# Three weight tiles in place of one, and a later start with a closer spacing for the norms of chunk 3, in a kernel that computes attention and a gated linear unit side by side

## The chip, the cores and the metric

The kernel runs on one core of a Trainium2 chip. The metric is the device time of one execution in microseconds (us). Before the change it is 309.67 us, the median of three runs (309.5, 309.67 and 310.33). In the profile, PE is TensorE's matmul row, PEld its weight loads, DVE is VectorE, ACT is ScalarE, POOL is GpSimd, and SP is SyncE, which here only issues DMAs.

## What is computed

There are 2048 rows `x` of width 640, in bf16. The rows are normalised, and two branches that both read the normalised rows are added to `x`:

```python
xn = layernorm(x)                      # (x - mean) / sqrt(var + 1e-5)
q, k, v = split(xn @ wqkv)             # 32 heads of width 20
p = softmax(mask(q @ k.T * 20**-0.5))  # causal, window of 256 positions
a = (p @ v) @ wo
b = (sigmoid(xn @ w_gate) * (xn @ w_up)) @ w_down   # inner width 1536
out = x + a + b
```

## The kernel before

**Tiling.** The 2048 positions are four chunks of 512 (chunks 0 to 3), each of four row blocks of 128. For one chunk the work is: the norms (DVE and POOL), which leave four row blocks `xn` (L273); the turning of each `xn` into the transposed tile `xnT` (four DMA transposes from SP's queue, L284; for chunk 0 it is done on PE, L280); the Q and K products (L300), whose results go to scratch in DRAM (`st`, L308) and come back spread over partitions (L318); the V products (L329); the scores and their exponentials (L490, L496), masks on POOL (L507) and, in one step of five, on DVE (L500, tile `edge`); the products with V (`acc`, L523); the GLU's gate and up products (`pg` L414, `pu` L421), whose tanh is on ACT (L417) and whose product `h` is on DVE (L425); and the output stage `g_out`, which for each row block adds twelve products of `h` with `w_down` (L435) and five with `wo` (L442) for either half of the columns (`y`), adds the row block of `x` on DVE (`rows`, L446) and stores it (L457).

**Order.** Instructions are issued on each engine in the order in which the Python program emits them. The main loop goes through the steps of the scores. Between two steps it pulls other work from a list, `fill`, whose entries (L692 to L710) are generators: each `yield` hands back the PE nanoseconds that were just emitted, and the loop goes on pulling until a budget (`APART`, 1800 ns, with a credit) is used up. `mix(a, b, first, every)` puts one pull of generator `b` behind every `every`-th yield of `a`, from yield number `first` on. The planner counts only the costs that `a` yields, so pulls of `b` at cost 0 do not change which PE work is emitted where.

**The norms.** `g_norms(c, turn)` (L346) emits the statistics of four row blocks, one per pull, then three pulls that emit nothing, then four `xn`, one per pull. For chunk 3 `turn` is false, and the transposes are a generator of their own, `g_turns(3)`, behind the norms. Chunk 3's norms begin in the entry `gu1b` (L704), which computes the GLU products 7 to 11 of chunk 1: ten yields, so ten pulls, four with statistics, three empty, three with an `xn`. The fourth `xn` and the four transposes come in `out1` (L705), the output stage of chunk 1, at every third yield. In the middle of its first row block `out1` also computes the first GLU product of chunk 2. The entry behind `out1` is `qk3`, the first that reads the transposed tile of chunk 3.

**The weights.** Q, K and V weights are one tile `wqkv` of 128 partitions by 5 by 1920 (L142). Four DMAs fill it: V's two halves (`load_v`, L159), then Q and K (`load_wqkv`, L150). PE's weight load for the second product of the first Q block waits for the load of K; the products of K have no wait on a DMA. 

Quoted lines, from `g_norms` and from the list:

```python
        for _ in range(3):
            yield 0
...
    norms3 = g_norms(3, False)
...
    fill.add("gu1b", mix(g_gu(1, 7, 12), norms3, 0, 1, False), 5 * GU)
    fill.add("out1", mix(g_out(1, g_gu(2, 0, 1)), itertools.chain(norms3, g_turns(3)), 1, 3), OUT + GU)
    fill.add("qk3", g_qk(3), 50 * MM)
```

PSUM tiles of one bank (`pg`, `pu`, `y`, `acc`, `pqk`, `pv`) share four buffers, `ps_d`; SP's DMAs go through one queue, in order of their issue.

Of the kernel before, what the change touches and what calls it, by code (L numbers as in the profile page):

```python
# [9 lines left out]
P = 128  # L10
S = 2048
D = 640
# [3 lines left out]
DC = D // P  # L16
# [9 lines left out]
HALF = 320  # L26
# [11 lines left out]
BF16 = mybir.dt.bfloat16  # L38
# [55 lines left out]
def kernel(  # L94
# [11 lines left out]
    nc = tc.nc  # L106
# [4 lines left out]
    def pool(name, bufs, **kw):  # L111
        return ctx.enter_context(tc.tile_pool(name=name, bufs=bufs, **kw))

    const = pool("const", 1)
# [24 lines left out]
        xc[c] = t  # L139
        nc.sync.dma_start(out=t, in_=xr[:, c * SBC:(c + 1) * SBC, :])  # L140

    wqkv = const.tile([P, DC, 3 * D], BF16, name="wqkv")  # L142
    wqkv_r = A_wqkv.rearrange("(c p) n -> p c n", p=P)
    wg = [const.tile([P, DC, FS], BF16, name=f"wg{k}") for k in range(F // FS)]
    wu = [const.tile([P, DC, FS], BF16, name=f"wu{k}") for k in range(F // FS)]
# [2 lines left out]

    ones = nc.const_aps.tensor(1.0, [P, CW], BF16)
    def load_wqkv(part):  # L150
        nc.sync.dma_start(out=wqkv[:, :, part * D:(part + 1) * D],
                          in_=wqkv_r[:, :, part * D:(part + 1) * D])

    xc[0] = xp.tile([P, SBC, D], BF16, name="xc")

# [1 line left out]
        queue.dma_start(out=xc[0][:, s, :], in_=xr[:, s, :])  # L157

    def load_v(hf):  # L159
        a = 2 * D + hf * HALF  # L160
        nc.sync.dma_start(out=wqkv[:, :, a:a + HALF], in_=wqkv_r[:, :, a:a + HALF])

    load_rows(0, nc.sync)
    load_rows(1, nc.sync)
    load_rows(3, nc.sync)
    load_v(0)
    load_rows(2, nc.sync)
    load_v(1)
    load_wqkv(0)
    load_wqkv(1)  # L170

    scratch = {(w, k): tc.dram_tile([H * 32, CW], BF16, name=f"s{w}{k}")
# [89 lines left out]
    def ln_block(c, s, mv=None):  # L262
        return ln_mv(ln_half(c, s, 1, ln_half(c, s, 0)), mv)

    def rstd_blocks(mvs):
        rstds = lnp.tile([P, SBC], FP32, name="rstds", bufs=1)
        nc.gpsimd.tensor_scalar(out=rstds, in0=mvs[:, :, 1], scalar1=EPS, scalar2=None, op0=ADD)
        nc.gpsimd.tensor_tensor(out=rstds, in0=rstds, in1=neghalf, op=POW)
        return rstds

    def norm_block(c, s, mv, rstd):
        xn = lnp.tile([P, D], BF16, name="xn")
        nc.vector.tensor_scalar(out=xn, in0=xc[c][:, s, :], scalar1=mv[:, 0:1],  # L273
                                scalar2=rstd[:, 0:1], op0=SUB, op1=MULT)
        xns[c, s] = xn
# [7 lines left out]
    def turn_block(c, s):  # L283
        nc.sync.dma_start(out=xnT[c][:, :, s * P:(s + 1) * P], in_=xns.pop((c, s)), transpose=True)  # L284

    def new_xnT(c):
        xnT[c] = xtp.tile([P, DC, CW], BF16, name="xnT")


    qk = {}  # L290
    vt = {}

    def proj_block(w, c, m):


        base = 0 if w == "q" else D
        ps = ps_d.tile([P, CW], FP32, name="pqk", tag="d")
        for d in range(DC):
            wt = wqkv[:, d, base:base + D].rearrange("p (k m) -> p m k", m=DC)
            nc.tensor.matmul(ps, lhsT=wt[:, m, :], rhs=xnT[c][:, d, :],  # L300
                             start=(d == 0), stop=(d == DC - 1))
        st = stp.tile([P, CW], BF16, name="st")
        if w == "q":
            nc.vector.tensor_copy(out=st, in_=ps)
        else:
            nc.scalar.copy(out=st, in_=ps)
        dst = scratch[w, c % 2].rearrange("(h j) s -> h j s", j=32)
        nc.sync.dma_start(out=dst[:, 4 * m:4 * m + 4, :], in_=st)  # L308
# [17 lines left out]
    def project_v(c, s, hf, home=ps_d, tag="d"):  # L326
        ps = home.tile([P, CW], FP32, name="pv", tag=tag)
        for d in range(DC):
            nc.tensor.matmul(ps[:, 0:HALF], lhsT=xnT[c][:, d, s * P:(s + 1) * P],  # L329
                             rhs=wqkv[:, d, 2 * D + hf * HALF:2 * D + (hf + 1) * HALF],  # L330
                             start=(d == 0), stop=(d == DC - 1))
        return ps

# [7 lines left out]
    def proj_v(c, s, hf, copy):  # L341
        copy_v(c, s, hf, project_v(c, s, hf), copy)

    MM = 216

    def g_norms(c, turn):  # L346


        new_xnT(c)
        mvs = lnp.tile([P, SBC, nc.vector.BN_AGGR_DIM], FP32, name="mvs", bufs=1)  # L350
        for s in range(SBC):
            ln_block(c, s, mvs[:, s, :])
            if s == SBC - 1:
                rstds = rstd_blocks(mvs)
            yield 0
        for _ in range(3):
            yield 0
        for s in range(SBC):
            norm_block(c, s, mvs[:, s, :], rstds[:, s:s + 1])
            yield 0  # L360
            if turn:
                turn_block(c, s)

    def g_turns(c):
        for s in range(SBC):
            turn_block(c, s)
            yield 0

    def g_qk(c):
        for w in "qk":  # L370
            for m in range(DC):
                proj_block(w, c, m)
                if c == 0 and w == "q" and m == 1:
                    load_x(1)
                if c == 0 and w == "q" and m == 3:
                    load_gu(wu, B_w_up, 0, FS // 2)
                if c == 1 and w == "q" and m == 3:
                    load_wo()
                if c and w == "k" and m == 1:
                    spread("q", c, 0, GH)  # L380
                yield 5 * MM
        if c == 0:
            spread("q", c, 0, 2)
            spread("k", c, 0, 2)
            spread("q", c, 2, 4)
            spread("k", c, 2, 4)
# [19 lines left out]
    def part(w, d, f):  # L406
        k, first = divmod(f * P, FS)
        return w[k][:, d, first:first + P]

    def g_gu(c, f0, f1):  # L410
        for f in range(f0, f1):
            pg = ps_d.tile([P, CW], FP32, name="pg", tag="d")
            for d in range(DC):
                nc.tensor.matmul(pg, lhsT=part(wg, d, f), rhs=xnT[c][:, d, :],  # L414
                                 start=(d == 0), stop=(d == DC - 1))
            th = tp.tile([P, CW], FP32, name="th")
            nc.scalar.activation(out=th, in_=pg, func=TANH, scale=0.5)  # L417
            yield 5 * MM
            pu = ps_d.tile([P, CW], FP32, name="pu", tag="d")
            for d in range(DC):  # L420
                nc.tensor.matmul(pu, lhsT=part(wu, d, f), rhs=xnT[c][:, d, :],  # L421
                                 start=(d == 0), stop=(d == DC - 1))
            h = hp.tile([P, CW], BF16, name="h")
            ht[c, f] = h
            nc.vector.scalar_tensor_tensor(out=h, in0=th, scalar=1.0, in1=pu, op0=ADD, op1=MULT)  # L425
            yield 5 * MM
# [6 lines left out]
    def down(c, s, y, cut):  # L433
        for f in range(FC):
            nc.tensor.matmul(y[:, 0:cut[1] - cut[0]], lhsT=ht[c, f][:, s * P:(s + 1) * P],  # L435
                             rhs=wd[:, f, cut[0]:cut[1]], start=(f == 0), stop=False)
            if f % 6 == 5:
                yield 6 * 136
# [11 lines left out]
    def new_rows(c, s, name="rows", bufs=3, queue=nc.sync):  # L450
        rows = lnp.tile([P, D], BF16, name=name, bufs=bufs)
        queue.dma_start(out=rows, in_=xr[:, c * SBC + s, :])
        return rows
# [5 lines left out]
    def outp(c, s, ys, rows):  # L459
        for y, cut in zip(ys, HALVES):  # L460
            add_wo(c, s, y, cut)
        for y, cut in zip(ys, HALVES):
            add_x(y, cut, rows)
        store(c, s, rows)

    def g_out(c, between, ahead=()):
        nxt = new_rows(c, 0)
        for s in range(SBC):
            rows = nxt
            if s == 0:  # L470
                yield from ahead
            if s + 1 < SBC:
                nxt = new_rows(c, s + 1)
            ys = [ps_d.tile([P, CW], FP32, name=f"y{i}", tag="d") for i in range(2)]
            for y, cut in zip(ys, HALVES):
                yield from down(c, s, y, cut)
            if s == 0:
                yield from between
            outp(c, s, ys, rows)
            yield 10 * 136  # L480
# [117 lines left out]
    def mix(a, b, first, every=1, rest=True):  # L598

        for k, cost in enumerate(a):  # L600
            yield cost
            if k >= first and (k - first) % every == 0:
                yield next(b, 0)
        if rest:
            yield from b
# [74 lines left out]
    fill = Fill()  # L680
    GU = 10 * MM
    OUT = 4 * 34 * 136
    APART = 1800
    FIRST_PART = 1000
    def later(load, *args):
        load(*args)
        yield 0

    norms1 = g_norms(1, True)
    norms2 = g_norms(2, True)  # L690
    norms3 = g_norms(3, False)
    fill.add("gu0a", mix(g_gu(0, 0, 4), norms1, 4, 1, False), 4 * GU)  # L692
    fill.add("gu0b", mix(g_gu(0, 4, 12), norms1, 0), 8 * GU)
    fill.add("x2", later(load_x, 2), 0)
# [7 lines left out]
    fill.add("qk2", g_qk(2), 50 * MM)  # L702
    fill.add("v2", mix(g_v(2), g_gu(1, 3, 7), 0, 1), 40 * 136 + 4 * GU)
    fill.add("gu1b", mix(g_gu(1, 7, 12), norms3, 0, 1, False), 5 * GU)  # L704
    fill.add("out1", mix(g_out(1, g_gu(2, 0, 1)), itertools.chain(norms3, g_turns(3)), 1, 3), OUT + GU)  # L705
    fill.add("qk3", g_qk(3), 50 * MM)
    fill.add("v3", mix(g_v(3), g_gu(2, 1, 5), 0, 1), 40 * 136 + 4 * GU)
    fill.add("gu2", g_gu(2, 5, 12), 7 * GU)
# [38 lines left out]
    c = NCH - 1  # L747
# [62 lines left out]
```

## Time and profile before

| What | Value |
|---|---|
| runs | 309.5, 309.67, 310.33 us |
| the profiled execution | 309.64 us |
| its span, from the first to the last instruction | 307.9 us |
| outside the span | 1.7 us |
| granted TensorE clock, mean | 1.000 |
| busy share of the span: PE, DVE, ACT, POOL | 98%, 56%, 64%, 55% |
| output stage of chunk 1 on PE (`out1`) | from 153.43 to 178.39 us |
| first Q product of chunk 3 on PE | 178.74 us |

A page of the profile gives busy time and instructions of each engine, the span in 40 slices, the chain of work that ended last (followed back from the last instruction), and groups of instructions by line with what ended the idle time in front of them. The timeline view merges neighbouring instructions of one line; its columns are the start, the length of the merged piece, engine, line, operation, tiles, count, and in brackets the idle time in front with its releaser. The modelled end of a matmul lies after the start of the next one, so lengths of PE pieces are best read from start to start.

### The profile page before, as it was taken

How to read it: one execution, taken by the hardware profiler on the slowest of the kernel's cores; microseconds unless marked ns; L12 is line 12 of the kernel's file. 1: busy time of each engine (PE TensorE's matmuls, PEld its weight loads, DVE VectorE, ACT ScalarE, POOL GpSimd, SP SyncE). 2: the span in 40 equal slices, each digit the busy share in tenths (PEclk: the TensorE clock that was granted, in tenths of full speed). 3: DMA queues.
4: the chain of work that ended last, by engine and by line, in shares of the span. 5: the costliest groups of instructions: out<-in, count | busy, mean ns of one | idle time of the engine just before them, and what ended most of it. 6: DMA issues, size and time to landing. Idle time of an engine off the chain costs nothing.

```text
span 307.9 us, 9937 instructions
## 1 busy us (share of the span) xinstructions
PE 300.4 (98%) x4276; PEld 167.7 (54%) x4311; DVE 171.2 (56%) x339; ACT 198.4 (64%) x197; POOL 168.7 (55%) x308
## 2 busy tenths in 40 slices
PE   7999999999999999999999999999999999999995
PEld 3654444555657654554457654554546664444774
DVE  4633667648698364487946164383734536363523
ACT  6923877698854649888674547878585547688000
POOL 6000686687874828576672728457372937566000
PEclk9999999999999999999999999999999999999999
DMA  7997986984709363630015312650000200000202
GB/s 220 366 319 237 333 161 199 351 228 144 234 2 127 69 179 124 189 109 2 3 24 87 87 57 87 209 162 0 3 2 2 86 27 21 2 2 6 84 21 67
DMA packets 40460, 35.68 MB, mean 116 GB/s; under 512 B 10560, under 2 KB 39872, under 8 KB 40384
## 3 DMA queue, kind: packets, MB, share of 16 engines
q1 hardware_dynamic: 39552, 34.27, 38.6%
q10 hardware_dynamic: 864, 0.77, 0.8%
q8 instruction: 34, 0.56, 0.8%
q14 instruction: 10, 0.08, 0.1%
HBM read 23.63 MB, written 10.26 MB: 110 GB/s over the span
## 4 chain that ended last, share of the span: by engine, by line
PE 96%; issue 1%; DMA 1%; ACT 1%; DVE 0%; SPq 0%
PE y L435 18%; PE pu L421 17%; PE pg L414 17%; PE pqk L300 14%; PE ps L490 9%; PE pv L329 7%; PE y L442 7%; PE acc L523 6%; DMA xc<-in_A_x_dram 1%; PE pt L280 0%; ACT xn L620 0%; ACT xn L625 0%; DVE xn L631 0%; SPq L157 0%; ACT rstd L626 0%
## 5 line engine op out<-in xcount | busy, mean ns | idle before, releaser
L507 POOL TENSOR_SCALAR_AFFINE_SELECT pT<-pT 64x512 bf16<-64x512 bf16 (+1 forms) x256 | 157.1, 614 | 109.1 <-ACT pT L496 96.6
L496 ACT ACTIVATE pT<-ps 128x2048 bf16<-128x2048 f32 (+1 forms) x76 | 141.0, 1855 | 59.8 <-PE ps L490 57.9
L425 DVE SCALAR_TENSOR_TENSOR h<-th,pu 128x512 bf16<-128x512 f32 x48 | 32.8, 683 | 51.4 <-PE pu L421 44.9
L421 PE MATMUL pu<-xnT,wu 128*128 128x512 bf16 x228 | 59.0, 380 | 0.7 <-issue 0.2
L414 PE MATMUL pg<-xnT,wg 128*128 128x512 bf16 x226 | 58.5, 380 | 0.9 <-issue 0.3
L435 PE MATMUL y<-wd,h 128*128 128x320 bf16 (+2 forms) x396 | 56.8, 295 | 0.0
L300 PE MATMUL pqk<-xnT,wqkv 128*128 128x512 bf16 x191 | 45.4, 381 | 0.6 <-issue 0.2
L435 PEld LDWEIGHTS <-h 128*128 128x128 bf16 x396 | 36.7, 98 | 15.9 <-issue 1.8
L417 ACT ACTIVATE th<-pg 128x512 f32<-128x512 f32 x48 | 28.6, 595 | 15.5 <-PE pg L414 15.4
L414 PEld LDWEIGHTS <-wg 128*128 128x128 bf16 x240 | 22.3, 98 | 25.8 <-issue 2.0
L421 PEld LDWEIGHTS <-wu 128*128 128x128 bf16 x240 | 22.0, 98 | 25.5 <-issue 2.0
L300 PEld LDWEIGHTS <-wqkv 128*128 128x128 bf16 x200 | 22.5, 119 | 18.7 <-issue 1.4
L535 DVE STREAM_TRANSPOSE t<-acc 128x512 f32<-128x512 f32 x32 | 21.1, 696 | 20.1 <-PE acc L523 20.1
L490 PE MATMUL ps<-qT,kT 20*64 20x320 bf16 (+4 forms) x1440 | 32.1, 260 | 0.0
L490 PEld LDWEIGHTS <-kT 20*64 20x64 bf16 x1440 | 15.4, 103 | 24.9 <-issue 21.8
L446 DVE SCALAR_TENSOR_TENSOR rows<-y,rows 128x320 bf16<-128x320 f32 x30 | 14.4, 488 | 25.9 <-PE y L442 25.7
L547 DVE TENSOR_TENSOR on<-t,rec 128x320 bf16<-128x320 f32 (+4 forms) x48 | 27.8, 579 | 1.1
L329 PE MATMUL pv<-wqkv,xnT 128*128 128x320 bf16 x160 | 25.8, 300 | 0.0
L442 PE MATMUL y<-wo,oc 128*128 128x320 bf16 (+2 forms) x165 | 24.2, 295 | 0.0
L338 DVE CAST v<-pv 64x320 bf16<-64x320 f32 x29 | 14.1, 486 | 12.5 <-PE pv L329 12.3
L523 PE MATMUL acc<-pT,v 64*32 64x320 bf16 (+4 forms) x1440 | 19.7, 253 | 0.0
L523 PEld LDWEIGHTS <-v 64*32 64x32 bf16 x1440 | 16.2, 91 | 5.8 <-ACT pT L496 1.7
(48 smaller groups left out, 157.3 us busy)
## 6 DMA issues: line engine op xcount, KB each, us to landing
qT<-sq SPq DMA_DIRECT2D x16, 256.0 KB
kT<-sk SPq DMA_DIRECT2D x16, 256.0 KB
sq<-st SPq DMA_DIRECT2D x20, 128.0 KB
sk<-st SPq DMA_DIRECT2D x20, 128.0 KB
out_dram<-rows SPq DMA_DIRECT2D x15, 160.0 KB
wg<-in_B_w_gate_dram SPq DMA_DIRECT2D x4, 480.0 KB
wu<-in_B_w_up_dram SPq DMA_DIRECT2D x4, 480.0 KB
xc<-in_A_x_dram SPq DMA_DIRECT2D x3, 640.0 KB
```

Of the source, the lines that this page charges most:

```text
L300: nc.tensor.matmul(ps, lhsT=wt[:, m, :], rhs=xnT[c][:, d, :], start=(d == 0), stop=(d == DC - 1))
L329: nc.tensor.matmul(ps[:, 0:HALF], lhsT=xnT[c][:, d, s * P:(s + 1) * P], rhs=wqkv[:, d, 2 * D + hf * HALF:2 * D + (hf + 1) * HALF], start=( ...
L414: nc.tensor.matmul(pg, lhsT=part(wg, d, f), rhs=xnT[c][:, d, :], start=(d == 0), stop=(d == DC - 1))
L417: nc.scalar.activation(out=th, in_=pg, func=TANH, scale=0.5)
L421: nc.tensor.matmul(pu, lhsT=part(wu, d, f), rhs=xnT[c][:, d, :], start=(d == 0), stop=(d == DC - 1))
L425: nc.vector.scalar_tensor_tensor(out=h, in0=th, scalar=1.0, in1=pu, op0=ADD, op1=MULT)
L435: nc.tensor.matmul(y[:, 0:cut[1] - cut[0]], lhsT=ht[c, f][:, s * P:(s + 1) * P], rhs=wd[:, f, cut[0]:cut[1]], start=(f == 0), stop=False)
L442: nc.tensor.matmul(y[:, 0:cut[1] - cut[0]], lhsT=oc[c, m][:, s * P:(s + 1) * P], rhs=wo[:, m, cut[0]:cut[1]], start=False, stop=(m == DC - 1))
L490: nc.tensor.matmul(ps[a * U:(a + 1) * U, i, col * U:(col + n) * U], lhsT=qk["k", kc, o // GH][32 * i:32 * i + DH, o % GH + a, kb * U:(kb + ...
L496: nc.scalar.activation(out=pt[:, :, 0:width], in_=ps[:, :, 0:width], func=EXP, scale=SCALE)
L507: nc.gpsimd.affine_select(out=view, in_=view, pattern=[[0, HG], [0, n], [sign, U]], compare_op=GE, fill=0.0, base=base, channel_multiplier ...
L523: nc.tensor.matmul(acc[32 * i:32 * i + 32, q * U:(q + n) * U], lhsT=vt[kb][a * U:(a + 1) * U, u, h * VW:h * VW + 32], rhs=pt[a * U:(a + 1) ...
```

## The change

Two things are changed. `g_norms` gets a parameter for the number of empty pulls between statistics and `xn`; chunk 3 uses 6 instead of 3, and `out1` pulls from chunk 3's norms and transposes at every second yield instead of every third. And the weights of Q, K and V become three tiles `wq`, `wk`, `wv` of 128 by 5 by 640, filled by the same four DMAs in the same order.

```diff
-    wqkv = const.tile([P, DC, 3 * D], BF16, name="wqkv")
+    wqkv = [const.tile([P, DC, D], BF16, name="w" + part) for part in "qkv"]
...
     def load_wqkv(part):
-        nc.sync.dma_start(out=wqkv[:, :, part * D:(part + 1) * D],
-                          in_=wqkv_r[:, :, part * D:(part + 1) * D])
+        nc.sync.dma_start(out=wqkv[part], in_=wqkv_r[:, :, part * D:(part + 1) * D])
...
-        a = 2 * D + hf * HALF
-        nc.sync.dma_start(out=wqkv[:, :, a:a + HALF], in_=wqkv_r[:, :, a:a + HALF])
+        a = hf * HALF
+        nc.sync.dma_start(out=wqkv[2][:, :, a:a + HALF], in_=wqkv_r[:, :, 2 * D + a:2 * D + a + HALF])
...
-            wt = wqkv[:, d, base:base + D].rearrange("p (k m) -> p m k", m=DC)
+            wt = wqkv["qk".index(w)][:, d, :].rearrange("p (k m) -> p m k", m=DC)
...
-                             rhs=wqkv[:, d, 2 * D + hf * HALF:2 * D + (hf + 1) * HALF],
+                             rhs=wqkv[2][:, d, hf * HALF:(hf + 1) * HALF],
...
-    def g_norms(c, turn):
+    def g_norms(c, turn, gap=3):
...
-        for _ in range(3):
+        for _ in range(gap):
             yield 0
...
-    norms3 = g_norms(3, False)
+    norms3 = g_norms(3, False, 6)
...
-    fill.add("out1", mix(g_out(1, g_gu(2, 0, 1)), itertools.chain(norms3, g_turns(3)), 1, 3), OUT + GU)
+    fill.add("out1", mix(g_out(1, g_gu(2, 0, 1)), itertools.chain(norms3, g_turns(3)), 1, 2), OUT + GU)
```

## The prediction

> **What bounds the kernel.** I read the page's busy shares first, then the chain that ended last, then the groups, and then only the stretch around `out1` in the chain, the timeline and the waits. On the page:
>
> ```profile
> PE 300.4 (98%) x4276; PEld 167.7 (54%) x4311; DVE 171.2 (56%) x339; ACT 198.4 (64%) x197; POOL 168.7 (55%) x308
> ...
> PE 96%; issue 1%; DMA 1%; ACT 1%; DVE 0%; SPq 0%
> ...
> L300 PE MATMUL pqk<-xnT,wqkv 128*128 128x512 bf16 x191 | 45.4, 381 | 0.6 <-issue 0.2
> L435 PEld LDWEIGHTS <-h 128*128 128x128 bf16 x396 | 36.7, 98 | 15.9 <-issue 1.8
> ```
>
> PE is 96% of the chain, and nearly all of its groups have no idle time in front that anything but "issue" ends. So the kernel is bound by PE from about 7 us on, and an edit that leaves PE's instructions alone can gain only where PE waits. The instruction lists of the two kernels show PE in the same order, matmul for matmul. What changes is: on DVE the place of the four `xn` of chunk 3; on SP the place of their four transposes; and one wait on PE, that for the load of K. The question is thus where PE waits for these three.
>
> The chain through the start of `out1`:
>
> ```profile
> 153.50 1.60 PE y L435 x11
> 155.10 0.04 issue
> 155.14 1.12 PE y L435 x7
> ```
>
> Twelve products make one `y`, and the break is in front of the twelfth: it needs the last `h` of chunk 1. DVE's timeline there, and the weight load:
>
> ```profile
> 152.63 0.65 DVE L425 SCALAR_TENSOR_TENSOR h<-th,pu 128x512 bf16<-128x512 f32 x1
> ...
> 152.78 0.59 ACT L417 ACTIVATE th<-pg 128x512 f32<-128x512 f32 x1
> ...
> 153.20 1.30 DVE L273 TENSOR_SCALAR xn<-xc,mvs,rstds 128x640 bf16<-128x640 bf16 x2
> ...
> 154.42 0.67 DVE L425 SCALAR_TENSOR_TENSOR h<-th,pu 128x512 bf16<-128x512 f32 x1
> 155.01 1.41 DVE L273 TENSOR_SCALAR xn<-xc,mvs,rstds 128x640 bf16<-128x640 bf16 x2
> 155.14 0.79 PEld L435 LDWEIGHTS <-h 128*128 128x128 bf16 x7 [0.38 <-DVE h L425]
> ```
>
> Two `xn` stand ahead of that `h` on DVE. It ends at 154.42 + 0.67 = 155.09, and PE goes on at 155.14. How long PE lost is read from start to start, against the same 18 products followed by scores in the third row block:
>
> ```profile
> 153.43 2.84 PE L435 MATMUL y<-wd,h 128*128 128x320 bf16 x18
> 156.20 0.42 PE L490 MATMUL ps<-qT,kT 20*64 20x320 bf16 x16
> ...
> 168.13 2.62 PE L435 MATMUL y<-wd,h 128*128 128x320 bf16 x18
> 170.67 0.42 PE L490 MATMUL ps<-qT,kT 20*64 20x320 bf16 x16
> ```
>
> 156.20 - 153.43 = 2.77 us here, 170.67 - 168.13 = 2.54 us there: 0.23 us.
>
> **The norms on DVE.** The new order is: both last `h` of chunk 1, two `xn`, the `h` of chunk 2, the third `xn`, the two `rows` of the first row block, the `edge` mask, the fourth `xn`. The last `h` now only needs its tanh, done at 152.78 + 0.59 = 153.37, and ends near 153.4 + 0.67 = 154.1. The twelfth product wants it at 153.43 + 11 x 0.136 = 154.93 (0.136 is 2.46 us / 18, the 18 products from 174.48 to 176.94). So it is 0.8 us early, and the stall of **0.23 us** goes. All later times of PE move up by that much; nothing else is late at this place, because the next waits on DVE (`y` banks) are further on.
>
> The first two moved `xn` fall into idle DVE time: the profile shows 3.39 us idle in front of the `h` at 159.81. The third now stands between that `h` and the `rows`. Before: `h` 159.81 to 160.50, `rows` at 160.88 and 161.56, to 162.05, `edge` from 162.04 to 162.46. After, with 0.23 taken off: `h` to 160.27, `xn` to 160.93 (660 ns, the mean of its group) or 161.18 (906 ns, its longest), first `rows` to 161.42 or 161.67, second to 161.9 or 162.16, `edge` no later than 162.6. Behind these `rows` wait the banks of the `acc` products, which start at 163.08 - 0.23 = 162.85, and `edge` is read later within them. Even the longest `xn` leaves 0.7 us, so I cost it at **0**; cover gone, it would cost PE what an `xn` has over 0.66 + 0.95, about 1.6 us. Below nothing it cannot go, as PE does not wait there. The fourth `xn` lies in front of a wait for `acc` that idles DVE 1.95 us: **0**.
>
> **The transposes on SP.** Before, they are issued at these places:
>
> ```profile
> 153.85 1.23 SPq L284 DMA_TRANSPOSE xnT<-xn  x1
> 162.08 0.36 SPq L457 DMA_DIRECT2D out_dram<-rows  x1
> 162.49 0.41 SPq L452 DMA_DIRECT2D rows<-in_A_x_dram  x1
> 162.96 2.54 SPq L284 DMA_TRANSPOSE xnT<-xn  x2
> 168.69 0.34 SPq L457 DMA_DIRECT2D out_dram<-rows  x1
> 169.08 0.43 SPq L452 DMA_DIRECT2D rows<-in_A_x_dram  x1
> 169.56 1.21 SPq L284 DMA_TRANSPOSE xnT<-xn  x1
> ```
>
> After: store, load, transpose 1, store, transpose 2, load, transposes 3 and 4, store, store. The second store waits for `rows` and goes at 168.46; transpose 2 is issued from 168.9 to 170.1, the load of the last row block to 170.5, transposes 3 and 4 to 173.1 (1.23 each, with gaps). The load comes 1.0 us later than before and is read at 177.82, so that is hidden. For the landing, the trace's DMA completion records: the pair issued from 162.96 to 165.50 landed at 165.78 and 168.13, 2.63 us behind the end of its issue; the single one of 169.56 landed at 172.40, 1.6 behind. So the fourth lands by 173.1 + 2.6 = 175.7 us. `qk3` starts at 178.74 - 0.23 = 178.5. Slack 2.8 us, cost **0**; past it every us costs one. Before, this slack was 6.3 us (178.74 - 172.40), so the change uses up more than half of it.
>
> Here a page of the Trainium skill speaks against the change. "VectorE: DVE Perf Modes", section "The three transpose paths", gives 1309 ns for a DMA transpose of 128 by 128 bf16; our tiles have five such blocks, an estimate by that page of 6.5 us each if the blocks go one after the other, and the last of three from 168.9 would land near 188.5, ten us late. The trace disagrees: the second of the pair landed 2.35 us behind the first. The sum goes by the rows.
>
> **The weights.** The wait for K moves from the second product of Q to the first of K, 25 products or 25 x 0.216 = 5.4 us later on PE. In this execution it held nothing: K had landed at 12.83 (completion records), the first Q product started at 13.20, and the group of L300 shows no idle time that a DMA ended. Gain **0**, and if K landed late in an execution, up to 5.4 us of lateness would now be hidden; no row shows that it does. Same weight loads, same products, same bytes; a load's rows in SBUF now lie side by side instead of 3,840 bytes apart. No row shows what that is worth. From above: PE's first V product starts at 6.96 and the first Q product at 13.20; 40 V products (5.44 us) and two turns by PE (8.40 to 8.68, 10.80 to 11.08: 0.56) fill 6.0 of these 6.24, so faster loads gain at most 0.24. From below: Q's 800 KB landed 2.3 us ahead of K's (10.53, 12.83); if V's two halves, 800 KB together, took a quarter longer, the first products would start 0.6 late. I take 0, since the packets are as many and as long, which is the nearest row (the same four loads, before).
>
> **Sum.** 309.64 (the profiled execution; 307.9 of span and 1.7 around it) - 0.23 + 0 + 0 + 0 = **309.41 us**. The profiled execution lies 0.03 below the median of the runs, 309.67.
>
> **Rivals.** A: the forecast, 309.4. B: the gain is given back or not made: the last `h` is held by something else, or the third `xn` delays the banks. For it, DVE is dense up to 154.4; against it, 0.8 and 0.7 us of slack. Time: **309.64**. C, the slower one: the transposes arrive late at `qk3`. Three of them are now issued behind the store of the second row block; it decides from the point where each takes over (178.5 - 168.9) / 3 = 3.2 us. Rows: 2.35 and 2.63 us speak against it. At twice the row, 4.7 us each, the last lands at 168.9 + 14.1 = 183.0, 4.5 late: **313.9**. C is the case that the Trainium skill's figure above speaks for; by that page's estimate the time would be 309.4 + 10 = about 319. D: the loads at the start go differently: **309.2** to **310.0** (309.41 - 0.24, 309.41 + 0.6). The change doing nothing that it says is B.
>
> **How the numbers follow.** A 0.62, B 0.21, C 0.07, D 0.07, and 0.03 for a gain that no view explains. 0.3% is 0.93 us, about what a measurement of this kernel can tell from no change: A, B and most of D are within it, C is slower, and 0.01 of D with it. So faster 0.03, same 0.89, slower 0.08. The range takes A, B, D's near part, and the spread of the runs of before below and above (309.5 to 309.67, once 310.33): 309.0 to 310.1.
>
> **What would show it.** Right: in the changed profile the first 18 products of `out1` take 2.54 us from start to start, the weight load of `h` has no wait for DVE, `acc` starts without a wait behind the third `xn`, and `qk3`'s first product without one for `xnT`. Wrong: a DMA-ended idle time at L297 at the start of `qk3` (C), a stall in front of `acc` (B), or a first V product well off 6.96 us (D).

## The result, and the profile after

The changed kernel takes 309.31 us (median of eleven runs, 309.01 to 310.45), the kernel before 310.21 us in the same comparison (eleven runs, 309.5 to 310.73). The ratio is 0.9975, 95% interval 0.9964 to 0.9986: a gain of 0.78 us, between 0.43 and 1.12, where 0.23 was forecast. (The medians alone are 0.90 us apart.)

The profiled execution of the changed kernel took 309.91 us, more than that of before (309.64). So the gain cannot be read from the two spans, and the places have to be compared one by one. From its page:

```profile
PE 300.0 (97%) x4276; PEld 167.5 (54%) x4311; DVE 170.7 (55%) x339; ACT 198.4 (64%) x197; POOL 168.7 (55%) x308
...
PE 96%; DMA 1%; issue 1%; DVE 1%; ACT 0%; SPq 0%
...
L297 PE MATMUL pqk<-xnT,wk 128*128 128x512 bf16 x97 | 23.1, 381 | 0.2
L297 PE MATMUL pqk<-xnT,wq 128*128 128x512 bf16 x94 | 22.8, 381 | 0.4 <-issue 0.2
```

PE is 96% of the chain as before, and neither the products of Q nor those of K wait for a DMA. The chain through the start of `out1`, where before broke off behind eleven products:

```profile
153.80 0.35 PE ps L487 x16
154.15 2.55 PE y L432 x18
156.71 0.35 PE ps L487 x16
```

The eighteen products are one piece of 2.55 us. In the timeline they go from 154.09 to the scores at 156.64, also 2.55 from start to start, against 2.77 in the first profile: the stall is gone. DVE there:

```profile
153.28 1.46 DVE L422 SCALAR_TENSOR_TENSOR h<-th,pu 128x512 bf16<-128x512 f32 x2
...
154.66 1.20 DVE L272 TENSOR_SCALAR xn<-xc,mvs,rstds 128x640 bf16<-128x640 bf16 x2
...
160.85 0.44 DVE L272 TENSOR_SCALAR xn<-xc,mvs,rstds 128x640 bf16<-128x640 bf16 x1
161.32 0.49 DVE L443 SCALAR_TENSOR_TENSOR rows<-y,rows 128x320 bf16<-128x320 f32 x1
162.00 0.49 DVE L443 SCALAR_TENSOR_TENSOR rows<-y,rows 128x320 bf16<-128x320 f32 x1 [0.19 <-PE y L439]
```

Both last `h` now stand together and end at 154.74; the third `xn` fits between the `h` and the first `rows` without moving the second, which still waits for PE. And SP's queue:

```profile
169.53 1.21 SPq L283 DMA_TRANSPOSE xnT<-xn  x1
170.84 0.53 SPq L449 DMA_DIRECT2D rows<-in_A_x_dram  x1
171.42 2.65 SPq L283 DMA_TRANSPOSE xnT<-xn  x2
```

The last two transposes landed at 175.27 and 175.80 (completion records); the first product of `qk3` started at 179.18, without a wait for them.

Why then is this execution longer than the one before? On PE, step by step against the first profile: the first V product starts 0.30 us later, because the first rows of `x` landed later (the DMA piece of the chain is 2.81 us, before 2.52); in the output stage of chunk 0 PE stands for 0.35 us between two products for no reason that the profile names; in `out1` 0.22 is won back. 0.30 + 0.35 - 0.22 = 0.43, the whole difference on PE from there to its last product. Of this 0.27 is left in the time, as what follows PE's last product took about 0.15 us less.

### The profile page after: what moved, and what is told of

Read it like the earlier page. It is cut to its first block, busy times and chain, and to the rows that moved or that the text cites. A ratio compares the mean times of both kernels' runs of the same rounds, so it can differ in the third digit from the quotient of the medians.

```text
span 308.2 us, 9938 instructions
## 1 busy us (share of the span) xinstructions
PE 300.0 (97%) x4276; PEld 167.5 (54%) x4311; DVE 170.7 (55%) x339; ACT 198.4 (64%) x197; POOL 168.7 (55%) x308
## 4 chain that ended last, share of the span: by engine, by line
PE 96%; DMA 1%; issue 1%; DVE 1%; ACT 0%; SPq 0%
PE y L432 18%; PE pu L418 17%; PE pg L411 17%; PE pqk L297 14%; PE ps L487 9%; PE pv L326 7%; PE y L439 7%; PE acc L520 6%; DMA xc<-in_A_x_dram 1%; PE pt L279 0%; ACT xn L617 0%; DVE xn L272 0%; DVE xn L628 0%; DVE stats L252 0%; SPq L156 0%
## 5 line engine op out<-in xcount | busy, mean ns | idle before, releaser
L326 PE MATMUL pv<-wv,xnT 128*128 128x320 bf16 x160 | 25.8, 300 | 0.0
L297 PE MATMUL pqk<-xnT,wk 128*128 128x512 bf16 x97 | 23.1, 381 | 0.2
L297 PE MATMUL pqk<-xnT,wq 128*128 128x512 bf16 x94 | 22.8, 381 | 0.4 <-issue 0.2
```

## The experiments

The ratios below are to the kernel before, with intervals. The question they had to settle is where the gain above 0.23 us comes from.

**The weights alone.** The changed kernel, with the norms as before:

```diff
-    norms3 = g_norms(3, False, 6)
+    norms3 = g_norms(3, False)
...
-    fill.add("out1", mix(g_out(1, g_gu(2, 0, 1)), itertools.chain(norms3, g_turns(3)), 1, 2), OUT + GU)
+    fill.add("out1", mix(g_out(1, g_gu(2, 0, 1)), itertools.chain(norms3, g_turns(3)), 1, 3), OUT + GU)
```

> The weights in three tiles, the norms of chunk 3 as before. Theory W (the part of the gain above the 0.23 us of the removed stall comes from the wait for K, which holds the second Q product in most executions though not in the profiled one): 0.4 to 0.7 us faster than before, ratio 0.9977 to 0.9987, and the first Q block of the profile runs without a gap. Theory N (the norms carry the whole 0.78 us, the stall in front of the twelfth product being longer in other executions): no change, ratio 0.9995 to 1.0005. Theory S (the rest is scatter between executions): no change. In this kernel's own profile the stall of 0.23 us at the start of the output stage of chunk 1 must still be there.

Measured: 310.25 us, ratio 0.9996 (0.9978 to 1.0013). My theory W falls: three tiles alone bring nothing that can be measured. The profile of this kernel held the better clue. PE's timeline at the start of `out1`:

```profile
154.88 1.67 PE L432 MATMUL y<-wd,h 128*128 128x320 bf16 x11
157.30 1.12 PE L432 MATMUL y<-wd,h 128*128 128x320 bf16 x7 [0.75 <-DVE h L422]
158.35 0.42 PE L487 MATMUL ps<-qT,kT 20*64 20x320 bf16 x16
```

158.35 - 154.88 = 3.47 us, where 2.54 is what the products need: the same stall, at the same product, is **0.93 us** here, and 0.23 in the first profile.

**The norms alone.** The kernel before, with the changed norms (and the parameter `gap` of `g_norms` that they need):

```diff
-    norms3 = g_norms(3, False)
+    norms3 = g_norms(3, False, 6)
...
-    fill.add("out1", mix(g_out(1, g_gu(2, 0, 1)), itertools.chain(norms3, g_turns(3)), 1, 3), OUT + GU)
+    fill.add("out1", mix(g_out(1, g_gu(2, 0, 1)), itertools.chain(norms3, g_turns(3)), 1, 2), OUT + GU)
```

> The norms of chunk 3 as in the changed kernel, the weights in one tile as before. Theory W: 0.23 us faster, ratio near 0.9993, and if this execution is one of the usual ones a gap between the first and the second Q product while K's load lands. Theory N: 0.78 us faster, ratio 0.9964 to 0.9986. Theory S: 0.23 us faster and no gap at the second Q product.

Measured: 309.32 us, ratio 0.9977 (0.9959 to 0.9995), the same as with both parts. PE's timeline at the start of `out1`:

```profile
154.97 2.62 PE L435 MATMUL y<-wd,h 128*128 128x320 bf16 x18
157.52 0.42 PE L490 MATMUL ps<-qT,kT 20*64 20x320 bf16 x16
```

The eighteen products take 157.52 - 154.97 = 2.55 us: no stall. The norms carry the gain, as theory N said, though this interval and that of the weights alone overlap.

**K's load late, with one tile and with three.**

```diff
     load_wqkv(0)
-    load_wqkv(1)
...
     load_gu(wu, B_w_up, 0, 0, FS // 2)
+    load_wqkv(1)
```

> One weight tile and the norms as before, but K's load is issued behind the first two loads of the GLU weights, 480 KB each. Two loads of 480 KB more in front of K put its landing from 12.8 to about 15.6 us (in the profile of before the second of these two landed at 15.64). Theory W: the second Q product, due at 13.4, waits until then, a gap of about 2.2 us in the first Q block, and the time grows by 1.5 to 2.2 us, ratio about 1.006. If the wait for K at the second Q product did not hold PE: no change.

> Three weight tiles, the norms as before, K's load issued behind the first two GLU loads. K lands at about 15.6 us, its first product is due at 18.6. Theory W: no gap in the first Q block, the time is that of the kernel with three tiles alone, 0.4 to 0.7 us faster than before. Theories N and S: as before, no change, since no wait is at stake there.

Measured: with one tile ratio 1.0102 (1.0064 to 1.0139), with three 0.9994 (0.9976 to 1.0012). PE's timeline with one tile:

```profile
13.02 0.38 PE L300 MATMUL pqk<-xnT,wqkv 128*128 128x512 bf16 x1
15.95 10.36 PE L300 MATMUL pqk<-xnT,wqkv 128*128 128x512 bf16 x40 [2.56 <-DMA wqkv<-in_A_wqkv_dram]
```

One product of Q, then 2.56 us of waiting for weights that Q does not use. So the wait is real, and three tiles take it away; but in the order of loads that both kernels have, K lands in time, and there is nothing to take. The ratio stands for a loss of 3.2 us, more than the 1.5 to 2.2 that were expected. It comes from four runs that differ: three of them (312.65, 312.91 and 313.32 us) lie 2.3 to 3.0 us above the median of before, 310.34, which is about the wait; the profiled one took 315.87 us, and in it the windows view gives a granted clock of 0.50 from 16 to 19 us, behind the pause. With three tiles the same late load costs nothing.

**The size of the stall.** Comparing the profile of the weights alone with that of before, instruction by instruction, all of DVE, POOL and ACT run alike between 125 us and 150.7, shifted by a constant. Then comes one pair. POOL and DVE in the kernel before (first profile):

```profile
150.73 0.89 POOL L507 TENSOR_SCALAR_AFFINE_SELECT pT<-pT 64x512 bf16<-64x512 bf16 x1
```

```profile
150.78 0.32 DVE L547 TENSOR_TENSOR on<-t,rec 128x192 bf16<-128x192 f32 x1
```

And the same two instructions with the weights alone (DVE's, the product of 128 by 192, is called the decisive product below):

```profile
152.18 0.66 POOL L504 TENSOR_SCALAR_AFFINE_SELECT pT<-pT 64x512 bf16<-64x512 bf16 x1
```

```profile
152.22 0.82 DVE L544 TENSOR_TENSOR on<-t,rec 128x192 bf16<-128x192 f32 x1
```

In both the select starts some 46 ns ahead. In one execution DVE goes through in 0.32 us and the select takes 0.89; in the other the select takes 0.66 and DVE 0.82. In either one of the two is held, by 0.50 us on DVE or by 0.23 on POOL, and nothing that the trace shows ahead of them differs by more than a few nanoseconds. From there on DVE is 0.50 us late, the first `xn` takes 800 ns instead of 587, and the last `h` comes 0.71 us later: 0.23 + 0.71 = 0.94, and the stall measured 0.93. The Trainium skill's page "SBUF — State Buffer", section "Who interferes with whom", states that VectorE and GpSimd share a port pair as an exclusive lock: a VectorE instruction with two SBUF inputs contends with a GpSimd instruction that reads SBUF, and the one that issues first has the pair for its whole length. The decisive product has two such inputs. The trace agrees that one is held: 0.32 against 0.82 us on one side and 0.66 against 0.89 on the other. The loser is late by somewhat less than the winner's time.

Whether the collision is needed for the stall was tried by leaving out the selects (the branch for steps without the `edge` mask), so that POOL's share of the span falls from 55% to 3%:

```diff
-        for (u, n), base, sign in ((step["diag"], 0, 1), (step["old"], -1, -1)):
-            ...
-                nc.gpsimd.affine_select(out=view, in_=view, ...)
         return pt, None
```

> The kernel before with POOL's mask selects of the scores left out, so that part of the mask is not computed; DVE's and PE's work is as before. Theory C (what makes the queue on DVE long enough is that its two-input products and its xn run beside POOL's selects: 0.82 us for a 128x192 product that takes 0.36 alone, 0.75 for an xn that takes 0.41 alone): the last h ends about 154.0 on the scale of before, no stall in front of the twelfth product, and the norms' place is worth nothing: this kernel and the next one within 0.1% of each other. Rival D (the queue is too long by its count of instructions, whatever POOL does): 0.2 us of stall or more here, and the next kernel faster by 0.07% or more.

> The changed kernel with POOL's mask selects left out, so that part of the mask is not computed. Theory C: the same time as the kernel before without the selects, within 0.1%. Rival D: faster than that by 0.07% to 0.3%. Either way no stall in front of the twelfth product.

Measured: the norms as before 309.68 us, ratio 0.9985 (0.9970 to 1.0000); the changed kernel 309.45 us, ratio 0.9974 (0.9960 to 0.9987). The intervals overlap, so the times do not tell C from D. The profiles do. The kernel before without the selects, DVE and then PE:

```profile
151.82 0.65 DVE L425 SCALAR_TENSOR_TENSOR h<-th,pu 128x512 bf16<-128x512 f32 x1
152.39 0.79 DVE L273 TENSOR_SCALAR xn<-xc,mvs,rstds 128x640 bf16<-128x640 bf16 x2
153.23 0.69 DVE L425 SCALAR_TENSOR_TENSOR h<-th,pu 128x512 bf16<-128x512 f32 x1
```

```profile
153.26 2.62 PE L435 MATMUL y<-wd,h 128*128 128x320 bf16 x18
155.81 0.42 PE L490 MATMUL ps<-qT,kT 20*64 20x320 bf16 x16
```

Two `xn` still stand ahead of the last `h`, and there is no stall: 155.81 - 153.26 = 2.55. The two `xn` take 0.79 us, where they took 1.30 in the first profile, and DVE's products ahead of them are shorter too: the last `h` ends 0.66 us behind the start of the eighteen products, in the first profile 1.66, and the twelfth needs it 1.5 us behind that start. Over the whole kernel the mean of an `xn` of the later chunks falls from 660 to 468 ns, that of a 128x320 product from 699 to 492. And from the first Q product to the end of PE's last one it is 291.0 us in both kernels without selects, 0.01 us apart, and 291.2 in the kernel before with them. Theory C holds for the stall.

**One `xn` ahead instead of two.** The changed kernel with `g_norms(3, False, 4)`.

> The changed kernel with 4 empty pulls instead of 6: one xn, not two and not none, stands ahead of the last h of chunk 1 on DVE. Theory Q (the stall in front of the twelfth product is what DVE still has to do ahead of that h: 0.93 us with two xn in most executions, of which one xn is 0.6 to 0.75): 0.2 to 0.35 us of stall, the time 0.2 to 0.35 us above that of the changed kernel, ratio to before 0.9978 to 0.9986. Rival F (the gain comes from the transposes going out elsewhere on SP, which are here as in the changed kernel): the same time as the changed kernel, ratio 0.9970 to 0.9978.

Measured: 309.75 us, ratio 0.9995 (0.9972 to 1.0019): inconclusive. In its profile the decisive product took 0.32 us, the lucky side, and the eighteen products took 157.57 - 155.02 = 2.55: with one `xn` and luck no stall is left. The other side was not profiled.

**The later start without the closer spacing.** The changed kernel with every third yield.

> The changed kernel with the norms and transposes taken up at every third yield of the output stage, as before: the later start alone. On SP two transposes then stand behind the store of the third row block and one behind that of the fourth, whose rows are ready at about 178.9 us; the last is issued by 180.4 and lands, 1.6 us behind the end of its issue, near 182. The first product of chunk 3 is due at 178.5. If the place of the transposes decides: PE waits 3.5 us or so for them, the time is 3 to 5.5 us above the changed kernel's, ratio to before 1.007 to 1.016, the more so if the granted clock falls after the wait as it did with K late. If the slack is larger than I worked out: as the changed kernel.

Measured: ratio 1.0123 (1.0091 to 1.0154). The chain around the start of `qk3`:

```profile
178.07 0.50 DVE rows L443
...
178.59 0.34 SPq L454
...
178.98 2.57 DMA xnT<-xn
...
181.59 2.35 PE pqk L297 x10
```

The last transpose waits behind a store in SP's queue, the store behind the last `rows` of chunk 1, and PE behind the transpose: 3.2 us. The profiled run, 312.45 us, is the shortest of four; the others took 314.55 to 314.69, and where they lost the further 2.1 us was not profiled. PE waiting for the transposes is rival C of the prediction, made to happen; the closer spacing turns a loss of 1.2% into the gain.

**The kernel before, profiled again.**

> The kernel before, unchanged, for another profile. Theory Q (the profile of before was one of the lucky executions; in most of them the last h of chunk 1 comes late by 0.9 us): the 18 products at the start of the output stage of chunk 1 take 3.4 to 3.5 us from start to start, where the first profile had 2.77. Rival: 2.77 us again, and the long stall belongs to the kernels with other loads at the start.

> The kernel before, unchanged, for a third profile: as for the one ahead of it, 3.4 to 3.5 us in most executions or 2.77 us in the lucky ones.

Measured: 309.27 and 309.37 us, and the eighteen products take 2.78 and 2.77 us. Both are on the lucky side, so "most executions" is not shown by profiles of this kernel. Nor does the rival fit, that other loads at the start make the long stall: the decisive product took 0.32 us in the changed kernel, with one `xn` ahead and with the late start alone, all with three tiles, and 0.82 us in the norms alone, with one tile. Over all kernels with selects that were profiled it was 0.32 us six times and 0.82 five times, with no rule in the layout. With the norms as before the long side cost 0.93 us (weights alone; 0.94 in both with K late), the short 0.23; with the changed norms the long side cost nothing. That is seen in the norms alone, whose eighteen products took 2.55 us with this product ahead of them (and in the warmer start below):

```profile
152.32 0.82 DVE L547 TENSOR_TENSOR on<-t,rec 128x192 bf16<-128x192 f32 x1
```

The times of all runs say more of the kernel before than its three profiles. In the four comparisons it ran 86 times: 36 runs took 309.3 to 310.0 us (median 309.61), 39 took 310.07 to 310.73 (median 310.31), and 11 more than 311. The two medians are 0.70 us apart, as the long stall and the short one are (0.93 - 0.23), and the three profiled executions (309.64, 309.27 and 309.37 us) go with the lower group. In the range of the upper one lie 8 of 22 runs with three tiles and the norms as before, but only 3 of 35 with the changed norms (the changed kernel, the norms alone, the warmer start). So the upper group is most likely the long side, though no execution of before in it was profiled. Its share is not fixed: 8 of 11 runs in the first comparison, then 18 of 29 and 11 of 29, and 2 of 17 in the one with these two profiles.

**A warmer start.** In the profile of the weights alone the first ten V products ran at half rate, 2.67 us in the chain against 1.44 in before. The clock records grant full speed at 10.06 us there and at 5.82 in before, and the first Q product came at 14.64 us instead of 13.20. The changed kernel got three more products of ones where PE idles (the counts were 6 and 4):

```diff
+    warm(6)
+    warm(5)
...
     for lo, hi in ((0, 3), (3, DC)):
         transpose_rows(0, act, lo, hi)
+    warm(2)
```

> The changed kernel with three more products of ones on PE at the start: one behind the ten, two between the turning of the first and of the second row block, where PE idles 0.5 us each. Theory G (the executions of 311 us and more are those in which the full TensorE clock is granted only near 10 us instead of 4.6 to 5.9, as the clock records of three profiles show, because PE idles too much between 5 and 7 us): full clock by 7 us at the latest, the slow group at 311 us goes or moves down by up to 1.3 us, the median as the changed kernel's or up to 0.2 us below, ratio to before 0.996 to 0.998. Rival H (the late grant does not depend on those idle times): a profile with a grant near 10 us again in some executions, the spread as before.

Measured: 309.31 us (308.89 to 310.09), ratio 0.9984 (0.9969 to 0.9998), before in that comparison 309.57 us. Full clock at 5.17 us in its profile, and no run above 310.1. No better than the changed kernel by its median; whether the late grants are gone is not shown, as there were only two runs near 311 among the 17 of before.

## Why the prediction was right, and which term was mis-sized

*PE's order is unchanged, only waits count*: right, the two lists of PE's products run side by side to the end of the span.

*The stall of 0.23 us goes*: right in place (the twelfth product) and in what ends it (the last `h`, behind two `xn`), too small in size in some executions. This is the mis-sized term of the sum. It was read to 0.01 us from one execution, and that execution stood on the short side of a collision between DVE and POOL, which the prediction does not name; on the long side the same term is 0.93 us. The measured 0.78 (0.43 to 1.12) lies between the two, which would mean that about eight in ten executions of before were on the long side ((0.78 - 0.23) / 0.70; three in ten at the interval's lower end). The times of before in that comparison fit the first: 8 of its 11 runs lie in the upper group, and 0.23 + 0.70 x 8/11 = 0.74. In the comparison of the last two profiles the same count would give 0.31. So the gain depends on how many executions of before fall on the long side. This reading of the times is an inference: in profiles, the long side with the norms as before has been seen only in kernels with three tiles or with K late. I had the hint in hand: `xn` from 407 to 906 ns in one group is no property of `xn`. I used the two ends for the third `xn` behind the change, and took the ones ahead of the stall as they stood in the trace.

*The time, 309.41 us*: near the measured 309.31, and partly by luck. The sum started from an execution on the short side, 309.64, and from there 0.23 is what the stall was worth. The prediction took that execution for a usual one, as it lies 0.03 below the median of three runs; over eleven runs the median of before is 310.21. One of the three, 310.33, already stood in the upper group.

*Third and fourth `xn` at 0, with 0.7 us of slack*: right. The third took 0.44 us and the second `rows` still waited for PE.

*Transposes at 0, last landing by 175.7 at the latest, slack 2.8*: right. It landed at 175.80 on a time scale that is 0.66 us later than the prediction's (the store of 168.46 was issued at 169.12), with 3.4 us to spare (179.18 - 175.80). The estimate worked out from the Trainium skill's page "VectorE: DVE Perf Modes", section "The three transpose paths", 6.5 us a tile one after the other, does not hold here: the last two landed half a microsecond apart.

*Weights at 0*: right within what was measured. Alone 0.9996 (0.9978 to 1.0013); the wait for K is real when K is late (2.56 us), and was not in force.

*Rival D, other loads at the start*: its sign, a first V product off 6.96 us, did come in the changed profile (7.26), but not as an effect of the change. Over all profiles that product starts between 6.76 and 7.30 us, with one tile and with three, and the first Q product at 13.0 to 13.5 us, or at 14.6 to 14.7 where the full clock was granted only near 10 us.

What stays open: a profile of before on the long side, why its share differs between comparisons, and the 0.35 us in the output stage of chunk 0 of the changed kernel's profile (0.14 in that of the warmer start, none in that of the norms alone).

## What to carry to other kernels

An engine that is late by a little at one product may be late by four times as much in another execution: look at the spread of an instruction's duration in its group, and where it is wide, price a stall with both ends. Here a VectorE instruction with two SBUF inputs beside a GpSimd select made such a spread (0.32 or 0.82 us); work that can move out of the queue ahead of a due result should, even if one profile shows hardly any stall. And when a producer is moved later, move with it the transfers behind it: the later start alone lost 1.2%.

## What the runs showed of the hardware

In all eleven profiles with selects POOL's select starts 45 to 48 ns ahead of the decisive product, and this ended either way: six times POOL was held, by 0.23 us, five times DVE, by 0.50. DVE was held where the lead was 47 or 48 ns, POOL where it was 45 to 47. So the order of the starts in the trace does not tell who was served first.

With one tile and K late, a pause of PE from 13.4 to 15.95 us came with 3.4 us at a granted clock of 0.50 (15.70 to 19.11 by the clock records). The Trainium skill's page "TensorE: Matmul & The Clock Gate", section "What's actually happening", has windows of 3.4 us in which PE's activity is judged. The trace agrees in the length. The length of the pause alone does not decide: with the later start alone PE waited longer, 3.20 us up to 181.59, and the granted clock stayed at 1.00.
